# Top-k attention and a hard-swish feed-forward block: exp shifts on ScalarE, late reads of h, one reciprocal per duo, and keys and queries transposed by DMA

## The chip, the cores and the metric

The kernel runs on one core of a Trainium2 chip. The metric is the device time of one execution in microseconds (us), lower is better. The kernel before takes 1581.66 us (median of three runs, 1581.61 to 1581.70). The profile quoted here is of one execution whose instructions span 1578.5 us. The engines are called by the profile's names: PE (matmul) with PEld (its weight loads), DVE (VectorE), ACT (ScalarE), POOL (GpSimd), and SP, the queue that issues DMAs.

## The reference

```
scores = (q @ k^T) / 8                      # 8 batches x 8 heads, 576 rows, head size 64
kth    = the 32nd largest of each row of scores
attn   = exp(scores - max) where scores >= kth, else 0;  attn /= sum + 1e-9
x      = attn @ v, heads side by side       # 4608 tokens x 512
h      = x @ w_in                           # 512 x 2048, float64 in memory, used as float32
out    = (h * clip(h + 3, 0, 6) / 6) @ w_out
```

Everything is float32 on the chip. The weights arrive as 64-bit floats and are turned into 32-bit floats by bit operations.

## The kernel before, in words

**Tiling.** Two heads are one Pair (128 partitions of head sizes). A Duo is two pairs and one tile of 128 query rows: `u` = 0, 1 names the pair, `t` = 0, 1 the head in it, and `sc[:, u, t*576:(t+1)*576]` is one head's row of scores. Each batch has 4 query tiles x 2 = 8 full duos, and 2 "rest" duos for the last 64 rows, where both heads share one 128-row tile (`nt` = 1, half the DVE work). There are 80 duos.

**Top-k on DVE.** `top(u, r)` runs four rounds for each `u`: MAX8 (L250) takes the 8 largest of a row, MATCH_REPLACE8 (L254) strikes them out; after round 3 the 32nd largest is known.

**After top-k,** for each `u`: `shift` (POOL, L263 and L266) makes scale*(kth - max); `exp` (ACT) runs a Prelu (L273), an Exp with a running sum (L278) and adds epsilon to the sum `den` (L283); `inverse` (DVE, L287) takes the reciprocal; `weights` (POOL) scales the row (L297) and splits it into 16-bit halves (L306); `flip` transposes the halves by the DMA crossbar (L312, SP); `join` puts the halves together again (L318, ACT for u = 0, POOL for u = 1); `values` multiplies by v (PE, L338) and `place` copies the result into xT (ACT, L348).

**Keys and queries.** `Pair.load` brings q and k by SP; `Pair.transpose` turns them with 9 PE transposes into the one PSUM tile `big` (L177), and ACT copies them out (L179 to L183).

**Feed-forward.** When xT of 128 tokens is whole, `queue` adds a block of 16 pieces: 8 pieces compute h in four groups of 512 columns (PE, L365; after each, ACT reads h twice, L373 and L375; POOL's gate, L379 and L380, comes two pieces later) and 8 pieces compute acc (PE, L385), whose output ACT scales (L395). The PSUM pool `ps_w` has three buffers, for h, acc and pv.

**Order.** The order is written out by hand. The loop runs over 80 duos x 8 slots; a slot is one round of top-k (`top(i // 4, i % 4)`). The tables `usual`, `behind`, `early`, `soon` say at which slot, counted from the duo's first, each part of that duo is put into its engine's queue. `scores` of duo m+1 goes in at slot 1 of duo m. At the end of a slot, `due` decides how many feed-forward pieces follow: 1 while any are left, 1 1/8 from 24 left, 1 1/4 from 48, half of that in rest duos. Engines take their own queue in order, so a waiting instruction holds all behind it.

**Weights.** `convert_step`, once a slot in the first 30 or so, converts a chunk of 512 columns: ACT (L108, L111), POOL (L109), DVE (L117, L118), POOL (L123).

Of the kernel before, what the change touches and what calls it, by code (L numbers as in the profile page):

```python
# [16 lines left out]
TOP_K = 32  # L17
# [12 lines left out]
def kernel(  # L30
# [62 lines left out]

    WC = 512

    def convert(dst, src):

        st = kqpool.tile([P, 2 * WC], U32, tag="kq", name="st")
        nc.sync.dma_start(st[:], src)
        yield
        words = st[:].rearrange("p (n two) -> p n two", two=2)
        lo, hi = words[:, :, 0], words[:, :, 1]
        a = gpool.tile([P, WC], F32, tag="g", name="a")
        y = gpool.tile([P, WC], F32, tag="g", name="y")
        nc.scalar.activation(a[:], hi.bitcast(F32), AF.Abs)  # L108
        nc.gpsimd.tensor_scalar(a[:], a[:], HI_MOST, HI_LEAST, ALU.min, ALU.max)  # L109

        nc.scalar.activation(y[:], lo, AF.Copy, bias=2.0, scale=2.0**-51)  # L111
        yield

        au, yu = a[:].bitcast(U32), y[:].bitcast(U32)
        nc.vector.tensor_scalar(au, au, 3, None, ALU.logical_shift_left)  # L117
        nc.vector.scalar_tensor_tensor(  # L118
            out=yu, in0=hi, scalar=0x80000000, in1=yu,
            op0=ALU.bitwise_and, op1=ALU.bitwise_or,  # L120
        )
        yield
        nc.gpsimd.tensor_tensor(  # L123
            dst.bitcast(I32), a[:].bitcast(I32), y[:].bitcast(I32), ALU.add
        )

    def weight_chunks():
# [11 lines left out]
    class Pair:  # L139
# [3 lines left out]
            self.b, self.hp = b, hp  # L143
            self.vm, self.vr, self.kr = vms[hp], vrs[hp], krs[b % 2 * NHP + hp]

        def load(self):
            h0 = 2 * self.hp
            t = self.landed = kqpool.tile([P, 2 * J + 1, 2, D], F32, tag="kq", name="landed")
            for i, src in enumerate((k, q)):
                for hh in range(2):  # L150
                    nc.sync.dma_start(
                        t[:, i * J : (i + 1) * J, hh, :],
                        src[self.b, h0 + hh, 0:JP, :].rearrange("(p j) d -> p j d", j=J),
                    )
                nc.sync.dma_start(
                    t[i * R : (i + 1) * R, 2 * J, :, :],
                    src[self.b, h0 : h0 + 2, JP:S, :].rearrange("h s d -> s h d"),
                )
# [12 lines left out]
        def transpose(self):  # L171
            kq = kqpool.tile([P, JP + S], F32, tag="kq", name="kq")
            self.kT, self.qT = kq[:, 0:JP], kq[:, JP : JP + S]
            ps = big()
            for j in range(2 * J + 1):
                rows = self.landed[:, j, :, :].rearrange("p h d -> p (h d)")
                nc.tensor.transpose(ps[:, j * P : (j + 1) * P], rows, ident[:])  # L177
            c0 = 2 * JP
            nc.scalar.copy(kq[:, 0:c0], ps[:, 0:c0])  # L179
            nc.scalar.copy(kq[:, c0 : c0 + R], ps[:, c0 + R : c0 + 2 * R])  # L180
            for hh in range(2):
                d = slice(hh * D, (hh + 1) * D)
                nc.scalar.copy(self.kr[d, hh, :], ps[d, c0 : c0 + R])  # L183

    class Duo:

# [72 lines left out]
        def shift(self, u):  # L259

            nt, m = self.nt, self.m[u]
            d = self.less[u] = mpool.tile([P, 2], F32, tag="shift", name="shift")
            nc.gpsimd.tensor_tensor(  # L263
                d[:, 0:nt], m[:, 0:nt, TOP_K - 1], m[:, 0:nt, 0], ALU.subtract
            )
            nc.gpsimd.tensor_scalar_mul(d[:, 0:nt], d[:, 0:nt], scale)  # L266

        def exp(self, u):

            nt, m = self.nt, self.m[u]  # L270
            for t in range(nt):
                row = self.row(u, t)
                nc.scalar.activation(  # L273
                    row, row, AF.Prelu, bias=m[:, t, TOP_K - 1 : TOP_K], scale=-1.0, alpha=FLAT
                )
            for t in range(nt):
                row = self.row(u, t)
                nc.scalar.activation(  # L278
                    row, row, AF.Exp, bias=self.less[u][:, t : t + 1], scale=-scale / FLAT,
                    accum_out=self.den[:, u, t : t + 1],  # L280
                )
            d = self.den[:, u, 0:nt]
            nc.scalar.activation(d, d, AF.Copy, bias=EPS)  # L283

        def inverse(self, u):
            d = self.den[:, u, 0 : self.nt]
            nc.vector.reciprocal(d, d)  # L287

        def weights(self, u):

# [61 lines left out]
    def feed_forward(xT, rows):  # L352
# [6 lines left out]
        for f0 in range(0, NFC, nf):  # L359
            h = ps_w.tile([P, 512], F32, tag="w", name="h")  # L360
            for f in range(f0, f0 + nf):
                if f == f0 + nf // 2:
                    yield None
                for i in range(NHP):
# [4 lines left out]
                        start=(i == 0),  # L369
                        stop=(i == NHP - 1),  # L370
                    )
            g = gpool.tile([P, 512], F32, tag="g", name="g")
            nc.scalar.activation(g[:], h[:], AF.Relu, bias=three[:], scale=1.0)  # L373
            hs = hpool.tile([P, 512], F32, tag="h", name="hs")
            nc.scalar.copy(hs[:], h[:])  # L375
            gs.append(g)

            def gate(g=g, hs=hs):
                nc.gpsimd.tensor_scalar(g[:], g[:], 6.0, 0.0, ALU.min, ALU.max)  # L379
                nc.gpsimd.tensor_tensor(g[:], g[:], hs[:], ALU.mult)  # L380

            yield gate
        acc = ps_w.tile([P, DM], F32, tag="w", name="acc")
        for f in range(NFC):
            nc.tensor.matmul(  # L385
                acc[:],
                gs[f // nf][:, f % nf * P : (f % nf + 1) * P],
                w_out[:, f, :],
                start=(f == 0),
                stop=(f == NFC - 1),  # L390
            )
            if f % 2 == 1:
                if f == NFC - 1:
                    o = opool.tile([P, DM], F32, tag="o", name="o")
                    nc.scalar.mul(o[:], acc[:], 1.0 / 6.0)  # L395
                    for p0, p1, dst in rows:
                        nc.sync.dma_start(dst, o[p0:p1, :])
                yield None

# [3 lines left out]
    for b in range(B):  # L405
        halves = [pairs[b][0:2], pairs[b][2:4]]
        for qt in range(J):
            duos += [Duo(h, qt) for h in halves]


            if qt == (0 if b == B - 1 else J - 1) and not 2 < b < B - 1:
                duos += [Duo(h, J) for h in halves]
            elif 2 < b < B - 1 and qt % 2 == 0:
                duos.append(Duo(halves[qt // 2], J))
# [5 lines left out]
    todo = []  # L420
    blocks = []
    left = 0
    gates = []

    def piece(count=1):
        nonlocal left
        for _ in range(count):
            while todo:
                try:
                    gates.append(next(todo[0]))  # L430
                    left -= 1
                    break
                except StopIteration:
                    todo.pop(0)
            else:
                gates.append(None)
            if len(gates) > 2:
                gate = gates.pop(0)
                if gate:
                    gate()  # L440

    def queue(*block):
        nonlocal left
# [42 lines left out]
    def land(count=1):  # L486

        for _ in range(min(count, len(chunks))):
            c = convert(*chunks.pop(0))
            next(c)  # L490
            landing.append(c)

# [17 lines left out]
    def pair_at(m, first):  # L510
# [2 lines left out]
        return pairs[b + 1][at - first] if b + 1 < B and 0 <= at - first < NHP else None  # L513

    first = pairs[0]
    first[0].load()
    land(2)
    first[1].load()
    first[0].transpose()
# [10 lines left out]


    usual = dict(
        shift0=3, exp0=4, inverse0=9, weights0=10, flip0=12, join0=15,
        shift1=7, exp1=8, inverse1=13, weights1=14, flip1=16, join1=19, values=22, place=23,
    )

    behind = dict(usual, values=25, place=26)
    early = dict(
        shift0=3, exp0=3, inverse0=4, weights0=4, flip0=5, join0=8,
        shift1=7, exp1=7, inverse1=8, weights1=8, flip1=9, join1=12, values=12, place=13,  # L540
    )
    soon = dict(
        shift0=3, exp0=3, inverse0=5, weights0=5, flip0=7, join0=10,
        shift1=7, exp1=7, inverse1=9, weights1=9, flip1=11, join1=14, values=16, place=17,
    )
    queued = {}
    for m in range(ND):
        for part, at in (early if m < 2 else soon if m >= ND - 2 else behind if per_batch <= m < ND - 4 else usual).items():
            queued.setdefault(8 * m + at, []).append((m, part))

    def parts(slot, late=None):

        for m, part in sorted(queued.get(slot, []), key=lambda x: x[1][:-1] != "shift"):
            if late is not None and (part[:-1] in ("inverse", "weights")) != late:
                continue
            if part == "values":
                values(m)
            elif part == "place":
                place(m)
            else:  # L560
                getattr(duos[m], part[:-1])(int(part[-1]))

    due = 0.0
    for m in range(ND + 3):
        u = duos[m] if m < ND else None
        for i in range(8):
# [16 lines left out]
                for p in duos[i // 4].pairs:  # L583
                    p.load_values()
            if i == 0:
                p = pair_at(m, 4)
                if p:
                    p.load()
            if i == 3 and u and u.pairs[0].b and 1 <= m % per_batch <= 2:
                for p in duos[m - 1].pairs:  # L590
                    p.load_values()
            if i == 5:
                p = pair_at(m, 5)
                if p:
                    p.transpose()

            due += ((left > 0) + (left >= 24) / 8 + (left >= 48) / 8) / (2 if u and u.rest else 1)
            piece(int(due))
            due -= int(due)
    while todo:  # L600
        piece()
    piece(2)

# [1 line left out]
_INS = ["q", "k", "v", "moe_w_in", "moe_w_out"]  # L605
# [30 lines left out]
```

## Time and profile before

| engine | busy, us | share of the span | what fills it |
|---|---|---|---|
| DVE | 1466.8 | 93% | MAX8 613.1 + 203.3, MATCH_REPLACE8 423.7 + 211.8, weights 55.0, reciprocals 24.6 |
| PE | 1456.9 | 92% | h 544.4, acc 516.9, pv 224.7, scores 220.7, transposes 41.5 |
| POOL | 1144.5 | 73% | weights of attention, gates, half of the joins, shifts 69.4 |
| ACT | 1096.3 | 69% | exp, scores copies, half of the joins, h reads 182.0 |
| DMA | | 43.5% of 16 engines | 160 crossbar transposes, loads, outputs |

Busy time is the union of an engine's instructions; the matmuls of PE overlap each other, so a PE that is busy all the time need not be at its peak. The idle time of an engine is put down to what ended it; what matters is the idle time of the engine that sets the pace.

### The profile page before, as it was taken

The numbers are of one execution on the slowest core, as the hardware profiler recorded it, in microseconds if no ns is written. First come the engines' busy times: TensorE is split into PE (matmuls) and PEld (weight loads), VectorE is DVE, ScalarE is ACT, GpSimd is POOL, SyncE is SP. The second block draws the span as 40 slices with busy tenths as digits, with TensorE's granted clock in tenths as the row PEclk, the third lists the DMA queues.
The fourth block names the chain that finished last, engine by engine and source line by source line (L and its number), as shares of the span: only waits on it lengthen the run. The fifth ranks groups of instructions, "written<-read, shape, count | busy, mean of one in ns | idle before, by whom it ended". The sixth has DMA issues, their size and how long they took to land.

```text
span 1578.5 us, 28787 instructions
## 1 busy us (share of the span) xinstructions
PE 1456.9 (92%) x10272; PEld 1039.0 (66%) x10272; DVE 1466.8 (93%) x3105; ACT 1096.3 (69%) x1865; POOL 1144.5 (73%) x1264
## 2 busy tenths in 40 slices
PE   5256799979999999998999999999999999999899
PEld 3153566567767777666777777776777767677675
DVE  6999999999999999999999999999999999999700
ACT  6675777777777777777776786777766787777621
POOL 4868687777867777867687777867687777767841
PEclk9568999989999999999999999999999999999999
DMA  8652543444344543545254543446244443533410
GB/s 236 159 181 45 113 83 81 94 91 97 76 90 89 101 83 76 101 85 119 55 106 76 97 89 82 93 93 116 57 96 87 98 88 74 103 65 68 83 22 14
DMA packets 450319, 144.49 MB, mean 92 GB/s; under 512 B 433280, under 2 KB 441472, under 8 KB 450176
## 3 DMA queue, kind: packets, MB, share of 16 engines
q1 hardware_dynamic: 450176, 142.65, 43.5%
q8 instruction: 81, 1.33, 0.3%
q14 instruction: 62, 0.51, 0.1%
HBM read 45.09 MB, written 9.44 MB: 35 GB/s over the span
## 4 chain that ended last, share of the span: by engine, by line
DVE 51%; PE 35%; POOL 5%; issue 3%; ACT 3%; DMA 1%; SPq 1%; POOLq 0%; ACTq 0%; DVEq 0%
DVE m L250 26%; DVE wk L254 22%; PE h L365 14%; PE acc L385 13%; PE pv L338 4%; PE big L232 3%; POOL e L306 1%; DVE y L118 1%; POOL sc L297 1%; DMA t<-e 1%; POOL eT L318 1%; DVE a L117 1%; PE big L177 1%; ACT sc L278 1%; ACT eT L318 1%
## 5 line engine op out<-in xcount | busy, mean ns | idle before, releaser
L250 DVE MAX8 m<-wk 128x8 f32<-128x576 f32 x864 | 613.1, 746 | 2.2
L385 PE MATMUL acc<-w_out,g 128*128 128x512 f32 x1152 | 516.9, 600 | 14.1 <-POOL g L380 14.1
L365 PE MATMUL h<-xT,w_in 128*128 128x128 f32 x4096 | 485.5, 279 | 17.3 <-ACT xT L348 17.3
L365 PEld LDWEIGHTS h<-xT,w_in 128*128 128x128 f32 x4096 | 475.0, 195 | 39.5 <-issue 18.2
L254 DVE MATCH_REPLACE8 wk<-m,wk 128x576 f32<-128x576 f32 x576 | 423.7, 742 | 0.0
L385 PEld LDWEIGHTS acc<-w_out,g 128*128 128x128 f32 x1152 | 213.6, 191 | 260.4 <-issue 238.6
L297 POOL TENSOR_SCALAR sc<-sc,den 128x576 f32<-128x576 f32 x288 | 213.8, 753 | 229.9 <-DVE den L287 222.7
L306 POOL COPY e<-sc 128x2304 uint16<-128x2304 uint16 (+1 forms) x192 | 320.3, 1678 | 10.2
L278 ACT ACTIVATE sc<-sc,shift 128x576 f32<-128x576 f32 x288 | 220.4, 769 | 40.5 <-POOL shift L266 37.7
L318 ACT COPY eT<-t 128x2304 uint16<-128x2304 uint16 (+1 forms) x82 | 215.9, 2632 | 37.9 <-DMA t<-e 35.3
L273 ACT ACTIVATE sc<-sc,m 128x576 f32<-128x576 f32 x288 | 210.1, 777 | 46.2 <-DVE m L250 46.0
L338 PE MATMUL pv<-eT,vm 128*64 128x128 f32 (+1 forms) x2560 | 164.0, 273 | 57.9 <-ACT eT L318 45.8
L254 DVE MATCH_REPLACE8 wk<-m,sc 128x576 f32<-128x576 f32 x288 | 211.8, 742 | 0.0
L318 POOL COPY eT<-t 128x2304 uint16<-128x2304 uint16 (+1 forms) x78 | 203.8, 2613 | 6.9 <-DMA t<-e 6.5
L338 PEld LDWEIGHTS pv<-eT,vm 128*64 128x64 f32 x2560 | 135.2, 141 | 109.3 <-ACT eT L318 49.7
L250 DVE MAX8 m<-sc 128x8 f32<-128x576 f32 x288 | 203.3, 742 | 2.4 <-ACT sc L236 2.4
L373 ACT ACTIVATE g<-h,three 128x512 f32<-128x512 f32 x144 | 98.5, 684 | 150.0 <-PE h L365 140.6
L380 POOL TENSOR_TENSOR g<-g,hs 128x512 f32<-128x512 f32 x144 | 185.0, 1285 | 12.1 <-POOL g L379 0.2
L233 ACT COPY sc<-big 128x2048 f32<-128x2048 f32 (+1 forms) x65 | 119.3, 1836 | 26.1 <-PE big L232 26.0
L232 PE MATMUL big<-kq 64*128 64x512 f32 x512 | 136.4, 653 | 0.0
L379 POOL TENSOR_SCALAR g<-g 128x512 f32<-128x512 f32 x144 | 89.2, 620 | 62.6 <-ACT g L373 52.4
L395 ACT ACTIVATE o<-acc 128x512 f32<-128x512 f32 x36 | 21.4, 595 | 106.6 <-PE acc L385 106.6
(47 smaller groups left out, 1113.1 us busy)
## 6 DMA issues: line engine op xcount, KB each, us to landing
landed<-in_k_dram SPq DMA_DIRECT2D x64, 128.0 KB, 3.0
landed<-in_q_dram SPq DMA_DIRECT2D x64, 128.0 KB, 3.0
st<-in_moe_w_in_dram SPq DMA_DIRECT2D x16, 512.0 KB, 5.1
vm<-in_v_dram SPq DMA_DIRECT2D x64, 128.0 KB, 2.3
st<-in_moe_w_out_dram SPq DMA_DIRECT2D x16, 512.0 KB, 6.6
out_dram<-o SPq DMA_DIRECT2D x32, 256.0 KB, 2.4
t<-e SPq DMA_TRANSPOSE x160, 4.6
landed<-in_k_dram SPq DMA_DIRECT2D x32, 32.0 KB, 2.8
```

The costliest lines, as they stand in the source:

```text
L232: nc.tensor.matmul(banks[:, 2 * i + hh, :], pr.qT[d, qs], pr.kT[d, :])
L250: nc.vector.max(self.m[u][:, t, 8 * r : 8 * r + 8], self.cur[t])
L254: nc.vector.match_replace(wk, self.m[u][:, t, 8 * r : 8 * r + 8], self.cur[t], LOWEST)
L273: nc.scalar.activation(row, row, AF.Prelu, bias=m[:, t, TOP_K - 1 : TOP_K], scale=-1.0, alpha=FLAT)
L278: nc.scalar.activation(row, row, AF.Exp, bias=self.less[u][:, t : t + 1], scale=-scale / FLAT, accum_out=self.den[:, u, t : t + 1],)
L297: nc.gpsimd.tensor_scalar(row, row, self.den[:, u, t : t + 1], 1.0, ALU.mult, ALU.mult)
L306: nc.gpsimd.tensor_copy(halves[:, :, to : to + c1 - c0], words)
L318: copy(eT[:, 0 : self.nb, :] .rearrange("p c q -> p (c q)") .bitcast(U16) .rearrange("p (x h) -> p h x", h=2), self.t16[u][:, 0 : 2 * self ...
L338: nc.tensor.matmul(pv[hh * D : (hh + 1) * D, u * w : (u + 1) * w], pr.vm[:, hh, c, :] if c < J else pr.vr[:, hh, :], rhs, start=(c == 0), ...
L365: nc.tensor.matmul(h[:, (f - f0) * P : (f - f0 + 1) * P], w_in[:, i, f * P : (f + 1) * P], xT[:, i, :], start=(i == 0), stop=(i == NHP - 1),)
L380: nc.gpsimd.tensor_tensor(g[:], g[:], hs[:], ALU.mult)
L385: nc.tensor.matmul(acc[:], gs[f // nf][:, f % nf * P : (f % nf + 1) * P], w_out[:, f, :], start=(f == 0), stop=(f == NFC - 1),)
```

## The change

It has six parts. (1) `shift` moves from POOL to ACT: one small ACTIVATE of both columns and one for each head. (2) ACT's two reads of h are put into its queue one piece later (`read`), so ACT does not stand at a matmul that is still running; the output's scaling (`write`) too. (3) One reciprocal and one epsilon addition serve both `u` of a duo (`inverse01`, `settle01`), and the slots of the tables move accordingly; `soon` holds for the last six duos, the last duo has a table of its own, and the rest duos of the last batch come one query tile later. (4) Batches 1 to 7 no longer use PE transposes: POOL splits the landed words in halves, the DMA crossbar transposes them, ACT joins them. Loads start one duo earlier. (5) The first 16 weight chunks keep one operand of their DVE step in PSUM. (6) The q part of the very first load is issued by ACT's queue.

```diff
-        y = gpool.tile([P, WC], F32, tag="g", name="y")
+        y = (
+            ps_w.tile([P, WC], F32, tag="w", name="yp")
+            if early
+            else gpool.tile([P, WC], F32, tag="g", name="y")
+        )
...
+        ys = gpool.tile([P, WC], F32, tag="g", name="ys") if early else y
-            out=yu, in0=hi, scalar=0x80000000, in1=yu,
+            out=ys[:].bitcast(U32), in0=hi, scalar=0x80000000, in1=yu,
...
+        def split(self):
+            self.e16 = kqpool.tile([P, 2 * (2 * J + 1) * P], U16, tag="kq", name="e16")
+            nc.gpsimd.tensor_copy(
...
+        def flip(self):
+            self.t16 = kqpool.tile([P, 2 * (2 * J + 1), P], U16, tag="kq", name="t16")
+            nc.sync.dma_start_transpose(self.t16[:], self.e16[:])
+        def join(self):
...
+            copy(kq[:, 0:c0], halves[:, :, 0:c0])
+            copy(kq[:, c0 : c0 + R], halves[:, :, c0 + R : c0 + 2 * R])
+            for hh in range(2):
+                d = slice(hh * D, (hh + 1) * D)
+                copy(self.kr[d, hh, :], halves[d, :, c0 : c0 + R])
...
-            nc.gpsimd.tensor_tensor(
-                d[:, 0:nt], m[:, 0:nt, TOP_K - 1], m[:, 0:nt, 0], ALU.subtract
-            )
-            nc.gpsimd.tensor_scalar_mul(d[:, 0:nt], d[:, 0:nt], scale)
+            nc.scalar.activation(d[:, 1, 0:nt], m[:, 0:nt, 0], AF.Copy, scale=-scale)
+            for t in range(nt):
+                nc.scalar.activation(
+                    d[:, 0, t : t + 1],
+                    m[:, t, TOP_K - 1 : TOP_K],
+                    AF.Identity,
+                    bias=d[:, 1, t : t + 1],
+                    scale=scale,
+                )
...
-        def inverse(self, u):
-            d = self.den[:, u, 0 : self.nt]
-            nc.vector.reciprocal(d, d)
+        def inverse(self, us):
+            d = self.den[:, us[0] : us[-1] + 1, 0 : self.nt]
+            nc.vector.reciprocal(d, d)
+        def settle(self, us):
+            d = self.den[:, us[0] : us[-1] + 1, 0 : self.nt]
             nc.scalar.activation(d, d, AF.Copy, bias=EPS)
...
+        reads.append(read)
+        if len(reads) > 1:
+            read = reads.pop(0)
+            gates.append(read() if read else None)
...
-    first[0].load()
+    first[0].load(nc.scalar)
...
     usual = dict(
-        shift0=3, exp0=4, inverse0=9, weights0=10, flip0=12, join0=15,
-        shift1=7, exp1=8, inverse1=13, weights1=14, flip1=16, join1=19, values=22, place=23,
+        shift0=3, exp0=4, shift1=7, exp1=8, settle01=8, inverse01=13, weights0=13, weights1=15,
+        flip0=15, flip1=17, join0=18, join1=20, values=22, place=23,
     )
...
     soon = dict(
-        shift0=3, exp0=3, inverse0=5, weights0=5, flip0=7, join0=10,
-        shift1=7, exp1=7, inverse1=9, weights1=9, flip1=11, join1=14, values=16, place=17,
+        shift0=3, exp0=4, shift1=7, exp1=8, settle01=8, inverse01=10, weights0=10, weights1=11,
+        flip0=12, flip1=13, join0=15, join1=16, values=18, place=18,
+    )
+    last = dict(
+        shift0=3, exp0=3, settle0=3, inverse0=5, weights0=5, flip0=7, join0=10,
+        shift1=7, exp1=7, settle1=7, inverse1=8, weights1=8, flip1=9, join1=11, values=11, place=11,
     )
...
-                p = pair_at(m, 4)
+                p = pair_at(m, 3)
                 if p:
                     p.load()
...
-            if i == 5:
-                p = pair_at(m, 5)
+            for at, first_at, part in ((2, 4, "split"), (5, 4, "flip"), (1, 5, "join")):
+                p = pair_at(m, first_at) if i == at else None
                 if p:
-                    p.transpose()
+                    getattr(p, part)()
```

## The prediction

> **What bounds the kernel now.** I read the page's busy times first: DVE 93%, PE 92%. Two engines tie, so the average settles nothing, and I cut the span at three points: the first MAX8 (13.6 us), the end of the weight conversion with duo 3 (144.1 us) and the last MAX8 (1491.3 us).
>
> ```profile
> core 0: us, PE busy (x) PEld busy (x) DVE busy (x) ACT busy (x) POOL busy (x), PEclk, DMA share, GB/s
> 0.00:13.60 13.60, 5.17 (x15) 2.66 (x15) 1.10 (x4) 5.16 (x10) 3.06 (x19) 1.00 0.76 183
> 13.60:144.10 130.50, 63.21 (x318) 43.04 (x318) 126.89 (x229) 89.50 (x148) 95.19 (x96) 0.71 0.54 160
> 144.10:1491.30 1347.20, 1309.51 (x9496) 938.35 (x9496) 1338.61 (x2874) 982.31 (x1677) 1014.55 (x1120) 0.99 0.45 88
> 1491.30:1578.50 87.20, 79.02 (x446) 54.92 (x444) 0.17 (x2) 19.30 (x33) 31.68 (x31) 0.98 0.10 23
> ```
>
> From 13.6 to 1491.3 us DVE idles 3.6 + 8.6 = 12.2 us of 1478. Its list of waits (us in total, times, longest) shows what it ever waited for:
>
> ```profile
> DVE a L117 <- POOL a L109: 13.3, 2, 10.0
> DVE den L287 <- ACT den L283: 9.3, 4, 6.7
> DVE m L250 <- ACT sc L236: 2.4, 2, 1.7
> ```
>
> 10.0 us of the first line and 1.7 of the third are the start, and 6.7 us of the second lie after the last MAX8; 6.6 us remain. So DVE sets the length up to 1491.3 us: full duos follow each other at 19.40 us, rest duos at 11.22 us, whatever PE does. PE is as full in these 1347 us, but scores are queued seven slots ahead, so PE may be late without stopping DVE, and it never stopped it. The chain of waits gives PE 35% of the span; that is a stretch in which PE and DVE run side by side.
>
> The last 87.2 us are PE's. Its timeline there (start, duration, idle before):
>
> ```profile
> 1495.72 1.81 PE L338 MATMUL pv<-eT,vm 128*64 128x128 f32 x16 [4.41 <-POOL eT L318]
> ...
> 1502.25 10.47 PE L385 MATMUL acc<-w_out,g 128*128 128x512 f32 x24
> 1512.65 1.09 PE L338 MATMUL pv<-eT,vm 128*64 128x128 f32 x16
> ...
> 1514.98 3.70 PE L385 MATMUL acc<-w_out,g 128*128 128x512 f32 x8
> 1518.52 14.45 PE L365 MATMUL h<-xT,w_in 128*128 128x128 f32 x128
> 1532.81 13.90 PE L385 MATMUL acc<-w_out,g 128*128 128x512 f32 x32
> 1546.55 14.45 PE L365 MATMUL h<-xT,w_in 128*128 128x128 f32 x128
> ```
>
> At 1495.72 PE waits for a join of duo 78: it had caught up with DVE. The pv of the last duo starts at 1512.65, and 34 pieces follow (2 of acc, then two whole blocks). A block takes 14.29 + 13.74 = 28.03 us between starts, a piece 1.753 us; 34 pieces are 59.6 us, and scaling and output take 3.8 us to the end. The sum is the tail: 21.3 + 2.3 (pv) + 59.6 + 3.8 = 87.0 us.
>
> So time = end of DVE's top-k (1491.3) + tail (87.2) + 3.2 us that the measured 1581.66 has over the span.
>
> **What the Trainium skill says.** SBUF — State Buffer, "Who interferes with whom": a DVE instruction with two SBUF inputs, or in a two-port mode, and a GpSimd instruction shut each other out for a whole instruction; with one SBUF input outside those modes DVE is not touched. The trace agrees: L118 (two SBUF inputs) takes 0.68 us alone and up to 1.75 us beside POOL. ScalarE: Activation LUTs, "What ACT_TABLE_LOAD costs": an ACTIVATE has a fixed 186 ns and some 93 ns more for a pointer operand; the two-column L283 here takes 0.20 us. TensorE: Matmul & The Clock Gate, "What's actually happening": an idle PE falls to half clock until it has been busy about 3.4 us. The trace agrees: 16 pv matmuls take 1.81 us after the 4.4 us gap, 1.09 otherwise.
>
> **The change, part by part.**
>
> *One reciprocal.* 160 reciprocals take 24.6 us of busy time, but they overlap their neighbours:
>
> ```profile
> 1425.12 0.74 DVE L254 MATCH_REPLACE8 wk<-m,sc 128x576 f32<-128x576 f32 x1
> 1425.78 1.41 DVE L250 MAX8 m<-wk 128x8 f32<-128x576 f32 x2
> ...
> 1427.90 0.74 DVE L254 MATCH_REPLACE8 wk<-m,wk 128x576 f32<-128x576 f32 x1
> 1428.56 0.15 DVE L287 RECIPROCAL den<-den 128x2 f32<-128x2 f32 x1
> 1428.63 1.40 DVE L250 MAX8 m<-wk 128x8 f32<-128x576 f32 x2
> ```
>
> From MATCH_REPLACE8 to the next MAX8 it is 0.66 us without a reciprocal and 0.73 with one: a reciprocal costs 0.07 us, not 0.154. 77 duos lose one (duos 0, 1 and the last keep both): 77 x 0.07 = **5.4 us** off DVE.
>
> *First load.* q's DMAs are issued from 2.8 to 4.8 us, behind those of k; the transposes that need q run at 6.67 us, DVE's first MAX8 at 13.59. On a second queue both go from the start: about **2 us** off, the q issue time (bounds 0 and 2.8).
>
> *y in PSUM.* The first 16 L118 lose one SBUF input, so POOL no longer shuts them out. Their excess over 0.68 us sums to 5.1 us (four of 1.75, two of 1.09). L117 stays in its two-port mode, and a stall may reappear there: I take **3.5 us** (bounds 0 and 5).
>
> *Shift on ACT.* POOL loses 69.4 us. ACT gains three small instructions for each full `u`, two for a rest `u`: 128 x 3 + 32 x 2 = 448 x 0.2 = 90 us at most, less where they overlap. This work lies beside DVE's next rounds. It removes the 37.7 us in which exp waited for the shift, which nobody on DVE felt. The wait that counted is the last: exp at 1496.14 instead of 1492.1, because POOL was at a join.
>
> *Reads a piece late.* ACT's 140.6 us at h and 106.6 us at acc become slack. They were in front of nothing that DVE needed in time, so directly 0; this pays for ACT's new work. A PSUM buffer stays taken one piece (1.75 us) longer, three buffers suffice for two h and a pv, and PE has the slack below.
>
> *Transposes.* 28 pairs x 9 leave PE: 1.15 us plus a gap of some 0.2, 28 x 1.3 = 36 us. In a batch, PE's 72 pieces (126.2), scores (8 x 2.45 + 2 x 2.6 = 24.8), pv (8 x 2.33 + 2 x 1.4 = 21.4) and transposes (5.2) make 178 us, and DVE's 8 x 19.40 + 2 x 11.22 also 178: PE has as much to do as DVE, afterwards 172. But pieces are dealt out by slots, and slots follow DVE. PE will idle more; nothing ends earlier for it. POOL gains 28 splits of about 2.1 us (price of L306), 59 us, for the 69 it loses. ACT loses 46 us of copies out of PSUM and gains 28 x (2.5 + 0.3 + 2 x 0.2), some 90 (price of L318, 2.80 us for 2304 words). In all ACT goes to about 1215 us, POOL stays. 28 more DMA transposes raise the DMA share from 44 to about 50%; the new chain has 4 slots from flip to join where a flip takes 4.6 us.
>
> *Slots.* I counted pieces through the loop with the new tables. At the end of top-k 26 pieces were left before and 25 will be, plus the last block of 16: the tail keeps its work. What moves is the order: before, 8 pieces stood ahead of the last pv and 34 behind it; now about 4 stand ahead and 37 behind. The last pv needs, from the last MAX8: shift and exp 4.2, reciprocal 0.2, POOL 3.6, flip 4.6, join 2.8 = 15.4 us. Four pieces and a pv last 9.3 us, so PE waits some 6 us and is slow for a moment after. Tail: 15.4 + 1.5 (second half of pv) + 37 x 1.753 (64.9) + 1 (cold clock) + 3.8 = 86.6, say **87 us**: no gain. The earlier last exp buys what the longer rest costs.
>
> *A risk on DVE.* `weights1` moves from slot 14 to 15 and `weights0` from 10 to 13, so both now follow one reciprocal. The scores of duo m+1 need the buffer (three of `sc`) that the split of duo m-2, u = 1, frees. Where two rest duos stand together (four places) slots last 1.4 us: POOL's 7 to 12 us for both `u` plus 2 us of copy end at slot 5 to 8, and DVE needs it at 8. Up to 3 us each. Against it, ACT comes to exp sooner, so the waits of 0.8, 1.4 and 0.7 us that DVE had around rest duos may go. I take 0 (bounds -3 and +12).
>
> Sum: 1491.3 - 5.4 - 2 - 3.5 + 0 = 1480.4. 1480.4 + 87 + 3.2 = 1570.6, given as **1570 us**, 0.7% faster.
>
> **Rivals.** *PE was the true bound* (0.08): PE runs full from 200 us to the end, and all 36 us come back: 1581.7 - 36, about 1545. For it: 92% and the chain. Against it: the 4.4 us gap at 1495.72, and DVE's unbroken 19.40. *The gain is lost to new waits* (0.12): the score buffers and the merged reciprocal cost DVE some 8 to 12 us, or the tail is 8 us longer as PE arrives late: 1579 to 1582. *ACT becomes the pace* (0.12): per full duo it has about 16 of 19.4 us, in rest duos about 10 to 12 of 11.2, and joins wait in its queue for transposes that now start later. If each of 16 rest duos costs DVE 1.5 us, 1570 + 24 = 1594, slower. Against it: ACT has five slots from exp to reciprocal, and its 250 us at matmuls are gone. The forecast has 0.68.
>
> **How the numbers follow.** All unknowns at their good ends (DVE 1473, tail 85) give 1561, at their bad ends (1491, tail 88) 1582; with the rivals the range is 1557 to 1581. Over 0.2% faster (below 1578.5): 0.68 + 0.08 and a little of the second rival, 0.78; same 0.08; slower 0.14.
>
> **What would show it.** Right: full duos at 19.33 us; last MAX8 near 1480; PE idle in the middle, and 5 to 8 us before the last pv; a tail of 85 to 89 us with two blocks and five pieces after it; DVE's waits under 10 us. Wrong: DVE waiting at L250 for scores or at the reciprocal beside rest duos; MAX8 slowed; a tail under 80 us, which would mean that late reads or freed PE time shorten it after all.

## The result, and the profile after

The changed kernel takes 1605.8 us (median, 1601.1 to 1606.5) against 1581.6 us: **1.5% slower**, ratio 1.0147 (95% interval 1.0128 to 1.0167). The forecast was 1570 us.

The span of the profiled execution is 1604.2 us. I cut it at the same three events as before: first MAX8, start of the fifth duo, end of the last MAX8.

```profile
core 0: us, PE busy (x) PEld busy (x) DVE busy (x) ACT busy (x) POOL busy (x), PEclk, DMA share, GB/s
0.00:13.30 13.30, 4.93 (x15) 2.79 (x15) 1.08 (x3) 5.07 (x10) 3.08 (x19) 1.00 0.76 192
13.30:134.50 121.20, 63.87 (x317) 42.97 (x317) 120.35 (x227) 90.92 (x169) 82.47 (x80) 0.75 0.58 172
134.50:1514.80 1380.30, 1295.74 (x9220) 919.50 (x9221) 1335.51 (x2798) 1094.68 (x2024) 1013.67 (x846) 0.97 0.51 98
1514.80:1604.20 89.40, 80.98 (x470) 55.76 (x468) 0.17 (x1) 22.63 (x35) 31.32 (x29) 0.98 0.11 23
```

The stretch of the weight conversion is shorter (121.2 us for 130.5), the tail is 2.2 us longer, and the loss is in the long middle: 1380.3 us for 1347.2, in which DVE was busy for 1335.5 us, 3.1 less than before. DVE idles 44.8 us there, where it idled 8.6. Its waits (us in total, times, longest) say for whom:

```profile
DVE den L328 <- ACT den L332: 38.8, 15, 6.2
DVE a L123 <- POOL a L114: 10.3, 2, 9.8
DVE m L287 <- ACT sc L273: 8.0, 6, 3.5
```

Before it was 9.3, 13.3 and 2.4 us. Without the start (9.8 us, and 1.7 us ahead of the first MAX8) and the wait after the last MAX8 (6.1 us), 39.6 us of waits lie in DVE's way, where there were 6.6: 33 us more. DVE's busy time fell by 9.7 us and the first MAX8 came 0.3 us sooner, so the last MAX8 should be some 23 us later; it is, 1514.8 for 1491.3.

By duos, most full duos take 19.34 to 19.36 us (before 19.40). Nearly all else that changed happens in **rest duos**: they took 11.22 us and now take 11.2 to 17.6. Their time over 11.2 us sums to 35.0 us over the sixteen, where it was 3.5. One of the longest waits, on DVE:

```profile
920.32 0.74 DVE L291 MATCH_REPLACE8 wk<-m,wk 128x576 f32<-128x576 f32 x1
926.92 0.18 DVE L328 RECIPROCAL den<-den 128x4 f32<-128x4 f32 x1 [5.86 <-ACT den L332]
927.02 0.73 DVE L287 MAX8 m<-wk 128x8 f32<-128x576 f32 x1
```

What ACT did in those microseconds, in its own order:

```profile
904.96 1.01 ACT L256 COPY sc<-big 128x1024 f32<-128x1024 f32 x1 [3.07 <-POOL e L351]
...
906.65 2.71 ACT L213 COPY kq<-t 128x2048 uint16<-128x2048 uint16 x2 [0.51 <-DMA t<-e]
909.23 0.67 ACT L213 COPY kr<-t 64x128 uint16<-64x128 uint16 x2
909.92 0.69 ACT L420 ACTIVATE g<-h,three 128x512 f32<-128x512 f32 x1
...
911.24 2.82 ACT L363 COPY eT<-t 128x2304 uint16<-128x2304 uint16 x1
913.90 0.22 ACT L300 ACTIVATE shift<-m 128x2 f32<-128x2 f32 x1
...
915.58 1.44 ACT L315 ACTIVATE sc<-sc,m 128x576 f32<-128x576 f32 x2
...
919.48 0.21 ACT L300 ACTIVATE shift<-m 128x2 f32<-128x2 f32 x1
...
923.14 0.59 ACT L422 COPY hs<-h 128x512 f32<-128x512 f32 x1 [2.36 <-POOL g L427]
923.62 1.44 ACT L315 ACTIVATE sc<-sc,m 128x576 f32<-128x576 f32 x2
...
926.62 0.21 ACT L332 ACTIVATE den<-den 128x4 f32<-128x4 f32 x1
```

The rest duo began on DVE at 912.2 us, so the row that the Prelu at 923.62 (the exp of u = 1 of the duo before) reads was ready then. ACT comes 11 us late: it stood 3.07 us for POOL's split of two duos earlier (the merged reciprocal's late weights), did 3.4 us of pair join (L213), 2.8 us of join (L363), shifts (L300) and reads (L420, L422) in nearly unbroken order, and stood again 2.36 us. Four of the six parts of the change are in this queue. Which of them cost what is a matter for runs.

### The profile page after: what moved, and what is told of

Read it like the earlier page. It is cut to its first block, busy times and chain, and to the rows that moved or that the text cites. A ratio compares the mean times of both kernels' runs of the same rounds, so it can differ in the third digit from the quotient of the medians.

```text
span 1604.2 us, 28295 instructions
## 1 busy us (share of the span) xinstructions
PE 1445.5 (90%) x10020; PEld 1021.0 (64%) x10020; DVE 1457.1 (91%) x3028; ACT 1213.3 (76%) x2236; POOL 1130.5 (70%) x972
## 3 DMA queue, kind: packets, MB, share of 16 engines
q1 hardware_dynamic: 514384, 158.88, 49.1%
## 5 line engine op out<-in xcount | busy, mean ns | idle before, releaser
L410 PE MATMUL h<-xT,w_in 128*128 128x128 f32 x4096 | 493.6, 282 | 29.2 <-ACT xT L393 21.4
L410 PEld LDWEIGHTS h<-xT,w_in 128*128 128x128 f32 x4096 | 480.6, 197 | 59.9 <-issue 25.9
L363 POOL COPY eT<-t 128x2304 uint16<-128x2304 uint16 (+1 forms) x78 | 203.6, 2610 | 165.2 <-DMA t<-e 165.1
L383 PE MATMUL pv<-eT,vm 128*64 128x128 f32 (+1 forms) x2560 | 168.2, 277 | 95.6 <-ACT shift L300 29.0
L383 PEld LDWEIGHTS pv<-eT,vm 128*64 128x64 f32 x2560 | 138.5, 143 | 144.8 <-ACT eT L363 37.9
L363 ACT COPY eT<-t 128x2304 uint16<-128x2304 uint16 (+1 forms) x82 | 215.9, 2632 | 0.9 <-DMA t<-e 0.4
L420 ACT ACTIVATE g<-h,three 128x512 f32<-128x512 f32 x144 | 98.2, 682 | 57.1 <-PE h L410 52.9
L269 PE MATMUL big<-kq 64*128 64x512 f32 x512 | 132.8, 638 | 0.0
L302 ACT ACTIVATE shift<-m,shift 128x1 f32<-128x1 f32 x288 | 72.5, 289 | 29.9 <-DVE m L287 25.2
```

The source lines that it names most:

```text
L269: nc.tensor.matmul(banks[:, 2 * i + hh, :], pr.qT[d, qs], pr.kT[d, :])
L363: copy(eT[:, 0 : self.nb, :] .rearrange("p c q -> p (c q)") .bitcast(U16) .rearrange("p (x h) -> p h x", h=2), self.t16[u][:, 0 : 2 * self ...
L383: nc.tensor.matmul(pv[hh * D : (hh + 1) * D, u * w : (u + 1) * w], pr.vm[:, hh, c, :] if c < J else pr.vr[:, hh, :], rhs, start=(c == 0), ...
L410: nc.tensor.matmul(h[:, (f - f0) * P : (f - f0 + 1) * P], w_in[:, i, f * P : (f + 1) * P], xT[:, i, :], start=(i == 0), stop=(i == NHP - 1),)
```

## The experiments

Each run is given as median and ratio to the kernel before (1580.3 to 1581.0 us beside these runs), with its 95% interval.

**Undoing one part of the changed kernel.**

*Two reciprocals* (tables usual and behind as before):

```diff
-        shift0=3, exp0=4, shift1=7, exp1=8, settle01=8, inverse01=13, weights0=13, weights1=15,
-        flip0=15, flip1=17, join0=18, join1=20, values=22, place=23,
+        shift0=3, exp0=4, settle0=4, inverse0=9, weights0=10, flip0=12, join0=15,
+        shift1=7, exp1=8, settle1=8, inverse1=13, weights1=14, flip1=16, join1=19, values=22, place=23,
```

> The changed kernel with two reciprocals and two epsilon additions a duo at the slots of before (exp0 4, inverse0 9, weights0 10, flip0 12, join0 15, inverse1 13, weights1 14, flip1 16, join1 19) in the tables usual and behind; the end tables and all else as changed. Theory A (the merged reciprocal puts both weights so late that ACT, in order, stands at the scores copy and at joins, and so reaches exp1 late in rest duos): DVE's waits fall from 47 us to under 15, time 1570 to 1580. Theory B (ACT has too much work of its own in rest duos: pair joins and shifts; the reciprocal of u = 1 stands at slot 13 as before): waits stay at 30 us or more, time 1595 to 1606.

1588.5 us, 1.0045 (1.0030 to 1.0060): 17.3 us of 1605.8 back, but not to 1580. Neither theory is enough alone.

*PE transposes* in place of split, flip and join, with the loads at their old slots too:

```diff
-            for at, first_at, part in ((2, 4, "split"), (5, 4, "flip"), (1, 5, "join")):
...
+            if i == 5:
+                p = pair_at(m, 5)
+                if p:
+                    p.transpose()
```

> The changed kernel with PE transposes of keys and queries at the slots of before in place of split, flip and join; all else as changed. Theory A (merged reciprocal): 1597 to 1606, the waits of DVE at the reciprocal stay over 25 us. Theory B (ACT's own work, 3.4 us of pair join that stands in front of exp in rest duos): waits fall under 20 us, time 1573 to 1588.

1591.6 us, 1.0065 (1.0048 to 1.0082): 14.2 us back. Both theories hold a part.

*Shift on POOL* again:

```diff
-            nc.scalar.activation(d[:, 1, 0:nt], m[:, 0:nt, 0], AF.Copy, scale=-scale)
...
+            nc.gpsimd.tensor_tensor(
+                d[:, 0, 0:nt], m[:, 0:nt, TOP_K - 1], m[:, 0:nt, 0], ALU.subtract
+            )
+            nc.gpsimd.tensor_scalar_mul(d[:, 0, 0:nt], d[:, 0, 0:nt], scale)
```

> The changed kernel with the two small POOL instructions for the shift as before; all else as changed. Theory A: within 4 us of 1605. Theory B: ACT sheds 0.65 us for each u, 1.3 us of the 7 us that five slots of a rest duo last; waits fall by 8 to 15 us, time 1590 to 1598.

1607.7 us, 1.0167 (1.0151 to 1.0182): nothing back, as theory A expected. With the other parts in place the shift comes late on POOL too: ACT stands 60.7 us at exp for it, where it stood 37.7 in the kernel before. What holds POOL up there was not traced.

*Reads at once:*

```diff
-        if len(reads) > 1:
+        if len(reads) > 0:
```

> The changed kernel with ACT's reads of h and the output's scaling queued at once, as before. Both theories: ACT stands at PE matmuls again, so it is later at exp; time 1605 to 1625. If the late reads themselves had put more work in front of exp in rest duos, it would be under 1600.

1608.6 us, 1.0171 (1.0150 to 1.0192): within what both theories expected, and within the noise of the changed kernel.

*Late weights:* two reciprocals at slots 9 and 13, but weights, flips and joins at the changed slots.

```diff
-        shift0=3, exp0=4, shift1=7, exp1=8, settle01=8, inverse01=13, weights0=13, weights1=15,
+        shift0=3, exp0=4, settle0=4, inverse0=9, shift1=7, exp1=8, settle1=8, inverse1=13,
+        weights0=13, weights1=15, ...
```

> The changed kernel with two reciprocals at the slots of before (9 and 13) and their own epsilon additions, but weights, flips and joins left at the changed slots (weights0 13, weights1 15, join0 18, join1 20). If the shared instruction itself makes DVE wait: about as with two reciprocals at the old slots, 1585 to 1592. If it is the late weights and joins on POOL and ACT (the scores copy then stands before the split of two duos earlier): 1600 to 1608.

1600.1 us, 1.0118 (1.0103 to 1.0133), at the lower edge of what the late weights were expected to cost. Of the 17.3 us that the merged reciprocal costs here, 11.7 (1600.1 - 1588.5) come with the late weights and joins that it brings, and 5.7, a small difference of two noisy medians, with the shared instruction.

**Undoing two, then three.**

> The changed kernel with both undone: two reciprocals at the old slots and PE transposes. Each alone took 14 to 17 us off. If both causes add up on the same queue of ACT, DVE's waits before the last duo fall from 38 us to under 8 us and the time is 1572 to 1580, the rest being the end tables; if they are the same microseconds twice, 1586 to 1592.

Two reciprocals and PE transposes together: 1593.9 us, 1.0084 (1.0069 to 1.0099), slower than either. A miss for both readings: the parts do not add. With two reciprocals the DMA transposes are a help. PE is busy 1438.2 us with them and 1465.7 us without, and ACT's waits for PE are 209.7 and 289.2 us.

> As the one with both undone, and with the end tables and the place of the last rest duos of before: what stays of the change is the shift on ACT, the late reads, the start (y in PSUM, q on ACT's queue). The start gives 9 us and the end tables cost some 6 us of waits of DVE and 2 us of tail: 1568 to 1574. If the end tables are neutral: 1575 to 1580.

Also the end of before: its tables, the place of the last rest duos, and the range of duos that use `behind`, which the change narrowed. What stays is shift on ACT, late reads and the start: 1586.2 us, 1.0032 (1.0020 to 1.0044). A miss, and an instructive one: the three parts that I had costed at a gain or at nothing still lose to the kernel before. So I turned round and added parts one at a time.

**Adding one part to the kernel before.**

*The start alone* (y of 16 chunks in PSUM, the first q on ACT's queue; the first two hunks of the diff):

> The kernel before with the changed start alone (y of 16 chunks in PSUM, first q on ACT's queue). The changed kernel reached its fifth duo 9.6 us earlier than before. If the start gives that: 1571 to 1574. If most of it came from the shift that left POOL in that stretch: 1576 to 1579.

1576.9 us, 0.9975 (0.9965 to 0.9985): **faster than both kernels**. DVE reaches its fifth duo at 139.9 us, in the kernel before at 144.1, in the changed kernel at 134.5. The rest of that lead comes with other parts, and little of it with the shift that left POOL (138.8 with the shift added, 136.6 with the merged reciprocal). In the changed kernel, this is line L124 up to 80 us (min/median/max in ns), and L118 of before:

```profile
L124 DVE SCALAR_TENSOR_TENSOR ys<-st,yp x15: 668/673/675, 17.4 to 70.1; 128x512 uint32<-128x512 uint32 x15
L124 DVE SCALAR_TENSOR_TENSOR y<-st,y x2: 1093/1425/1757, 73.5 to 77.7; 128x512 uint32<-128x512 uint32 x2
```

```profile
L118 DVE SCALAR_TENSOR_TENSOR y<-st,y x16: 675/682/1747, 16.9 to 77.2; 128x512 uint32<-128x512 uint32 x16
```

With one operand in PSUM none takes over 0.68 us, and the next two, with both in SBUF, take 1.09 and 1.76 us. The trace agrees with the Trainium skill, SBUF — State Buffer, "Who interferes with whom": a DVE instruction with at most one SBUF input, outside the two-port modes, does not contend with GpSimd.

On this base I added each of the others alone, by undoing all the rest in the changed kernel (the end tables with the later rest duos and the narrower `behind`):

> Added alone to the kernel before with the changed start (1576.9 us): the shift on ACT. If ACT's queue in front of exp1 in rest duos is what DVE waits for, 1.3 us more a duo there costs DVE 1 to 2 us at each of ten or so rest duos less what exp no longer waits for POOL: 1578 to 1586. If the late reads are what made the kernel with both undone slow, 1572 to 1577 (the last exp comes earlier).

> Added alone to the same base: the reads of h and the output's scaling queued one piece late. If late reads hold the PSUM buffer longer and put a read in front of exp in rest duos: DVE waits 10 us or more, 1582 to 1590. If they only remove ACT's standing at PE: 1572 to 1578.

> Added alone to the same base: one reciprocal and one epsilon addition a duo with the changed slots of weights, flips and joins in the tables usual and behind. If this alone delays ACT in rest duos: DVE waits 15 us or more less 5 us saved, 1585 to 1595. If it needs the other additions to hurt: 1572 to 1578.

> Added alone to the same base: keys and queries of batches 1 to 7 split by POOL, transposed by DMA, joined by ACT. If the join in ACT's queue alone delays exp in rest duos: 1583 to 1592. If it needs the merged reciprocal to hurt: 1572 to 1578. PE loses some 35 us of work in both cases.

> The base with the changed end alone: the tables soon and last, the rest duos of the last batch after query tile 1, and the changed range of behind. From the two kernels that differ only in this, 1593.9 against 1586.2: 1582 to 1587, with 3 to 7 us of waits of DVE in the last six duos and a tail about 3 us longer than 87. If the end tables cost only together with the late reads: 1575 to 1580.

| added to the base (1576.9 us) | us | ratio to before (interval) | cost | time over 11.2 us in rest duos |
|---|---|---|---|---|
| nothing | 1576.9 | 0.9975 (0.9965 to 0.9985) | | 4.0 us |
| shift on ACT | 1588.2 | 1.0048 (1.0033 to 1.0063) | +11.3 | 15.5 |
| merged reciprocal with its slots | 1584.5 | 1.0024 (1.0015 to 1.0034) | +7.6 | 15.4 |
| end tables | 1582.3 | 1.0004 (0.9996 to 1.0013) | +5.4 | 5.9, and a tail of 92.6 us |
| late reads | 1580.0 | 0.9995 (0.9986 to 1.0004) | +3.1 | 9.2 |
| DMA transposes | 1577.2 | 0.9978 (0.9970 to 0.9987) | +0.3 | 2.7 |

The sum, 1576.9 + 27.7 = 1604.6, is close to 1605.8; since the parts do not add, that is partly luck. Shift and late reads together, for example, are the kernel of 1586.2 us above: 9.3 us over the base, where their costs alone sum to 14.4. The +0.3 of the DMA transposes is within the noise. The late reads lie between the two expected ranges, the shift is over the expected 1578 to 1586 by 2 us, and the merged reciprocal just under its 1585 to 1595. The end tables cost mostly in the tail (92.6 us for 87.2).

Why does the shift cost most? It adds 0.66 us of work for each `u`. But see the waits of ACT, first of the base, then with the shift added:

```profile
ACT sc L278 <- DVE m L255: 48.3, 32, 4.0
ACT sc L283 <- POOL shift L271: 39.5, 27, 6.8
ACT eT L323 <- DMA t<-e: 36.2, 21, 4.8
```

```profile
ACT shift L302 <- DVE m L287: 100.6, 82, 5.6
ACT eT L363 <- DMA t<-e: 19.0, 9, 5.0
```

The shift stands at slots 3 and 7, where exp stands at 4 and 8; join0 of the duo before falls on slot 15, that is 7, and goes behind the shift. On POOL the shift waited for the last MAX8 while ACT could run the join; on ACT the shift waits in front of the join, and exp comes after both.

The order of the queue allows this account, but single rest duos show more. Here is one of them (duo 62, counted from 0, which starts on DVE at 1168.57 us in the base and at 1176.30 us with the shift), on ACT, first in the base, then with the shift:

```profile
1163.76 0.60 ACT L400 ACTIVATE o<-acc 128x512 f32<-128x512 f32 x1 [4.94 <-PE acc L390]
...
1169.55 2.80 ACT L323 COPY eT<-t 128x2304 uint16<-128x2304 uint16 x1 [1.06 <-DMA t<-e]
...
1173.25 1.46 ACT L278 ACTIVATE sc<-sc,m 128x576 f32<-128x576 f32 x2
```

```profile
1174.29 0.60 ACT L446 ACTIVATE o<-acc 128x512 f32<-128x512 f32 x1 [4.32 <-PE acc L434]
...
1179.16 0.48 ACT L302 ACTIVATE shift<-m,shift 128x1 f32<-128x1 f32 x2
1180.30 2.81 ACT L363 COPY eT<-t 128x2304 uint16<-128x2304 uint16 x1 [0.66 <-DMA t<-e]
...
1184.01 1.44 ACT L315 ACTIVATE sc<-sc,m 128x576 f32<-128x576 f32 x2
```

Both times ACT stands at PE's acc, and the join still waits for its transpose, so here the shift did not hold the join back. What moved is PE: against the start of the rest duo, acc is there 4.8 us ahead in the base and 2.0 us ahead with the shift, and all behind it is 3 us later. The four longest waits that the shift brings in rest duos all have such a stand at acc ahead of them, which ends 2.8 to 5.6 us later than in the base. PE in turn stood longer for ACT's copy of pv into xT (30.2 us in all for 17.5). So ACT and PE hold each other up; which of these delays comes first was not separated.

*Shift at the slots of exp:*

```diff
-        shift0=3, exp0=4, ... shift1=7, exp1=8,
+        shift0=4, exp0=4, ... shift1=8, exp1=8,
```

> The base with the shift on ACT, but queued at the slots of exp (4 and 8) in place of 3 and 7, in the tables usual and behind. If the cost of the shift is its place (ACT stands at it for the last MAX8, with a join of 2.8 us behind it that could have run): DVE's waits before the last duo fall from 18 us to under 6, time 1573 to 1579. If it is the work of the small instructions: 1585 to 1589 as before.

1581.4 us, 0.9999 (0.9991 to 1.0008): 6.8 of the 11.3 us come back, from 1588.2, a little short of the expected range. DVE's waits at the reciprocal fall from 19.0 to 11.9 us in all, and PE's for the copy into xT from 30.2 to 20.3 (the profile is of its slowest run, 1583.6 us). So the place in the queue is the larger share. Work alone does not explain the rest, as the next run shows.

> The base with the DMA transposes and with the shift on ACT at the slots of exp. If place was the cost: 1571 to 1578, a little under the base through the earlier last exp. If work was the cost: 1588 or more.

With DMA transposes besides: 1577.7 us, 0.9980 (0.9973 to 0.9987), level with the base. The same shift that costs 4.5 us beside PE transposes costs 0.5 beside DMA transposes (1577.2 without it), although ACT has more to do: it is busy 1227.2 us, more than in the changed kernel (1213.3). So the amount of ACT's work alone is not what makes DVE wait. What fell are PE's busy time (1435.4 us for 1458.1) and ACT's waits for PE (219.7 us for 270.1).

*Merged reciprocal apart from rest duos* (only for full duos that no rest duo follows within two, with DMA transposes):

```diff
+            when = usual if any(u.rest for u in duos[m : m + 3]) else merged
```

> The base with the DMA transposes and with one reciprocal and the changed slots only for full duos that no rest duo follows within two. If the merged reciprocal hurts only in rest duos: some 45 duos save 0.06 us each, 1572 to 1577. If it hurts everywhere: 1582 or more.

1595.7 us, 1.0091 (1.0072 to 1.0111): a clear miss, and worse than the merged reciprocal everywhere with PE transposes (1584.5). DVE waits 33.0 us at reciprocals, mostly in rest duos. In one of the longest waits (duo 42) POOL's late join of a merged duo runs until the next duo's early weights start, and ACT's join then stands 3.5 us for its transpose in front of exp; in another (duo 8) ACT stands 5.6 us at PE's acc. The merged reciprocal everywhere with DMA transposes was not run, so how much is the changing table and how much the company stays open.

*The reciprocal one slot later*, where the shift alone was added, and in the whole changed kernel:

```diff
-        ... inverse1=13, weights1=14, ...
+        ... inverse1=14, weights1=14, ...
```

```diff
-        ... inverse01=13, weights0=13, weights1=15,
+        ... inverse01=14, weights0=14, weights1=15,
```

> The base with the shift on ACT at its changed slots (1588.2 us), and the reciprocal of u = 1 at slot 14 in place of 13, in the tables usual and behind. If DVE only reached its reciprocal too early in rest duos: each of nine waits of 0.7 to 4.0 us shrinks by up to 1.4 us, 15 us of waits become about 6, time 1577 to 1582. If DVE waits for work that piles up on ACT, it waits as long one slot later: 1586 to 1590.

> The whole changed kernel with the one reciprocal of a duo at slot 14 in place of 13 and weights0 with it. If the slot helps: some ten waits in rest duos shrink by 1.4 us, 1590 to 1598. If the weights, now later still, delay the scores copy and the joins by as much: 1602 to 1610.

1590.0 us, 1.0056 (1.0039 to 1.0072), and 1608.2 us, 1.0173 (1.0155 to 1.0190): nothing gained. The waits of DVE in the first of them:

```profile
DVE den L328 <- ACT den L332: 12.2, 9, 3.7
DVE m L287 <- ACT sc L273: 10.6, 8, 1.7
```

At the reciprocal 6.8 us are gone (19.0 before the move), and 8.3 us have come up at the first MAX8 of the next duo (2.3 before). In ACT's queue the copy of the next scores stands right behind exp1 and `den`; if exp1 is late, so is the copy. The reciprocal was only the first place where DVE felt it. That speaks against my idea of a too early reciprocal: in rest duos **ACT's queue itself is late**. A fourth buffer for `sc`, which would take away the wait for POOL's split, was not tried.

## Why the prediction was wrong

**The step that failed** is the "+ 0" in the sum for DVE's end: the forecast priced the shift and the late reads at nothing there, as work beside DVE's rounds, and took 0 for the later slots of the merged reciprocal. Alone they cost 11.3, 7.6 (net of what it saves) and 3.1 us, mostly in rest duos, where DVE then waits for an ACT that comes late to exp. The last MAX8 was forecast near 1480.4 us and came at 1514.8. Of these 34 us, 33 are new waits of DVE; what DVE was to save came nearly in full (9.9 us of 10.9). The sign that the forecast named for being wrong, DVE waiting at the reciprocal beside rest duos, is what the profile shows. Term by term:

- *Bound and frame.* Time = end of top-k + tail held, and PE was not the bound: PE lost transposes, and DMA transposes added alone moved nothing (+0.3 us). But PE's lateness reaches DVE through ACT's queue, which the forecast left out.
- *One reciprocal*, 5.4 us: on DVE right in kind and too high (19.345 us for 19.40 a duo, where 19.33 was forecast; alone it takes 3.6 us off DVE's busy time), since a reciprocal of four columns takes a little more of DVE's time than one of two (0.08 us for 0.07). Its price elsewhere was put at 0 and is such that alone it loses 7.6 us net, and 17.3 us in company, most of it through late weights. "I take 0 (bounds -3 and +12)" for the risk in rest duos failed. The mechanism named there (POOL's split, then the scores copy, at slots of 1.4 us) is on the trace, with ACT standing 27.5 + 7.3 us at scores copies for POOL; but I weighed it for four places and for DVE's scores only, and put no price on what stands behind it in ACT's queue.
- *Shift on ACT*, "beside DVE's next rounds": wrong, +11.3 us alone. I costed its 90 us of work and not the wait that moved with it into ACT's queue, though the profile of before showed that wait (42.1 us of POOL at L263).
- *Reads a piece late*, "directly 0": +3.1 us alone. That ACT's 250 us at matmuls "are gone" was wrong too: its waits at h and acc fell from 247 to 117 us, and those at the scores of full duos rose from 26 to 102; in all it waited 284 us for PE, before 319. With the late reads alone on the base the same happens: 244 to 170, and 26 to 55 us.
- *y in PSUM*, 3.5 us: the start gives 4.1 us. *First load*, 2 us: 0.3 at most, and nothing in the run with the start alone (first MAX8 at 13.58 us for 13.59). q lands sooner but k later: in the changed kernel PE's nine transposes start at 5.57 us and end at 7.72; in the kernel before they started at 4.54 and ended at 7.97.
- *Transposes:* as forecast. ACT is busy 1213 us (forecast 1215), POOL 1131 (it was to stay at 1144), DMA 49.1% (50).
- *Tail*, 87 us: 89.4, 2.2 more than before. The order came as counted:

```profile
1527.91 1.09 PE L383 MATMUL pv<-eT,vm 128*64 128x128 f32 x16 [1.23 <-ACT eT L363]
...
1532.29 1.64 PE L383 MATMUL pv<-eT,vm 128*64 128x128 f32 x16 [3.06 <-POOL eT L363]
...
1534.28 9.74 PE L434 MATMUL acc<-w_out,g 128*128 128x512 f32 x20
1543.85 14.45 PE L410 MATMUL h<-xT,w_in 128*128 128x128 f32 x128
1558.14 13.90 PE L434 MATMUL acc<-w_out,g 128*128 128x512 f32 x32
1571.88 14.45 PE L410 MATMUL h<-xT,w_in 128*128 128x128 f32 x128
1586.17 13.90 PE L434 MATMUL acc<-w_out,g 128*128 128x512 f32 x32
```

Five pieces of acc and two blocks follow the last pv, 37 pieces. The second half of pv waits until 17.5 us after the last MAX8, not 15.4: on ACT a join of 2.78 us stands between the last shift (1514.81 us) and its exp (1517.66). Again ACT's queue.

The third rival, ACT as the pace (0.12), comes nearest: 1594 us with 1.5 us for each rest duo, where 31 us more than before were lost over sixteen, some 2 us each. Its reason, ACT's amount of work, is not what the runs show; late joins and the order of the queue are. Against this rival I had set five slots from exp to reciprocal. Five slots are 12 us in a full duo and 7 in a rest duo, and exp was not at the head of the queue. The second rival (8 to 12 us for the score buffers and the merged reciprocal) came true besides: 7.6 us net for the merged reciprocal alone.

Not settled: how much of ACT's lateness comes from its standing at PE, at POOL and at transposes, and why some parts cost more in company than alone (the merged reciprocal) and some less (shift and late reads).

## What to carry to other kernels

Before work or a wait is moved to an engine, look at what stands behind it in that engine's order where its slack is least, not on average: ACT was busy 69% over the span, and a wait moved into its queue cost 11 us, of which 7 came back when it was queued one slot later. A kernel in which ACT had more work, but in another order and beside a freer PE, was level with the base. Where a schedule is written in slots, check the slots that are short. And add parts one at a time to the kernel that was good; undoing one from a bundle that collides told far less.

## What was not expected of the hardware

A reciprocal of two columns lasts 0.15 us, but among its neighbours it delays the next MAX8 by only 0.07 us; one of four columns lasts 0.17 us and delays it by 0.08 (medians). So sharing one reciprocal saves DVE 0.06 us a duo. On this kernel an instruction of DVE with two SBUF inputs that POOL holds up shows as a longer instruction (1.75 for 0.68 us), not as idle time: DVE's 93% of busy time held microseconds that were really waits (some 5 us in the first sixteen chunks of weights).
